# First inverse steps in pairs, wider VectorE steps, one tile for x's two parts and a reload by halves, in a newly planned order

## The chip, the cores and the metric

The kernel runs on one core of a Trainium2 chip. The time is device time in microseconds for one execution; the profile of one execution, taken by the hardware profiler, gives its span and the start and duration of its instructions. In the profile PE is TensorE, DVE is VectorE, ACT is ScalarE, POOL is GpSimd and SP is SyncE.

## The reference

Two heads are computed from inputs of 2048 positions and 512 channels and put side by side.

```python
def _A_ref(x, dft_seq_re, dft_seq_im, dft_hid_re, dft_hid_im):
    a = einsum("bsd,ed->bse", x, dft_hid_re)
    b = einsum("bsd,ed->bse", x, dft_hid_im)
    return einsum("ts,bse->bte", dft_seq_re, a) - einsum("ts,bse->bte", dft_seq_im, b)

def _B_ref(u, log_A_real, A_imag, C_real, C_imag, log_dt, D_skip):
    dt = exp(log_dt); A = -exp(log_A_real) + 1j * A_imag
    C = (C_real + 1j * C_imag) * dt[:, None]
    P = exp((A * dt[:, None])[:, :, None] * arange(L)[None, None, :])
    K = 2.0 * einsum("dn,dnl->dl", C, P).real
    y = irfft(rfft(u_t, 2 * L) * rfft(K, 2 * L), 2 * L)[:, :, :L]
    return transpose(y) + u * D_skip
```

The first head is a Fourier mixing of x by four given matrices. The second convolves each channel of u with a kernel K that is a sum of 128 complex exponentials.

## The kernel before, in words

**Fnet** (the first head) works in 12 groups. Eight groups ("s") multiply x, transposed, with a block of the sequence matrices (the input `in_sT`), 16 items of 128 rows each, into four PSUM tiles `acc` of 128x512; the results `p` go to memory and come back. Four groups ("p") multiply the hidden matrices `w` with `p`, 8 items each. Every operand is fp32 and is split into a high part `hi` (a copy rounded to fp32r, on ScalarE, L233) and a low part `lo` (the difference, on VectorE, L238), and every product is made of three matmuls, high by high, low by high and high by low: 1920 matmuls at L405. x and w stay in SBUF, both parts; a block arrives as `raw` (L346 on ScalarE's queue for the very first, L350 on SyncE's for the others) and is split when it is due. At the end of a group, ScalarE copies `acc` into `y` (L419; L414 for the last), and a DMA stores it.

**Ssm** (the second head) uses two more PSUM tiles, `f0` and `f1`, for everything it does:

- Tables of exponentials, `t` (t1 and t2), in 16 chunks of 32 channels. Each is doubled step by step: VectorE multiplies the part there is by a factor (`mul`, L641, real and imaginary products into `prod`), and adds the two (`add`, L650).
- Taps (L838, 16 steps) multiply t1 by t2 into K. Stage 1 of the transform of K (L893, 8 steps) and of u (L956, 8 steps) go to memory.
- Quarters: four parts of 128 channels (h = 0 to 3), each with four quarters of the frequencies (q). One quarter is a stage-1 step (L1085, into both `f` tiles), ScalarE's copy of them into the tile `uk` (L1064), VectorE's products of the two spectra (L1069 and L1071, then the difference L1102 and the sum L1105), and the first inverse (L1112) into both `f` tiles, from which ScalarE copies into `z` (L1139, L1158). Two DMAs store each z to `zs`.
- When all quarters of a part h are stored, `zs` comes back as `zl`, and the second inverse follows: `inverse` (L1255) for h = 0 and 1, `inverse2` (L1216) for 2 and 3, with a sum and a difference on VectorE ahead of it (L1207, L1209). Its result goes out as `out_yb` (L1241).

For h < 3 the first inverse was made for one quarter at a time (32 matmuls), for h = 3 for two at a time (64 matmuls, `first_inverses`).

**The order.** Nothing is scheduled by the compiler: a planner written in Python (`Plan`) runs when the kernel is built. Each part of the work is a generator that asks for an engine with a cost in us and an urgency, or waits for an event or a semaphore. The planner gives the engine to the request that can start first, and instructions are emitted in that order on every engine. Its costs are the constants `HOP` (from one engine to another), `RESULT` and `LATENCY` (of a DMA), and the functions `act`, `dve` and `load`. Engines execute in order, so an instruction that waits holds those behind it on its engine. Of a DMA, it is the issue that stands in an engine's order: SyncE issues most of them, and ScalarE a few. DMAs of these two take turns on eight completion semaphores, so an issue also waits until the one eight issues earlier has landed.

Of the kernel before, what the change touches and what calls it, by code (L numbers as in the profile page):

```python
# [54 lines left out]
HOP, RESULT, LATENCY = 0.3, 0.15, 3.3  # L55
# [34 lines left out]
class Plan:  # L90
# [3 lines left out]
    def __init__(self):  # L94
        self.free, self.ready, self.now = {}, [], 0.0
        self.count, self.streaming = 0, True
        self.done, self.blocks, self.asked = 0, [], -9.0

        self.later, self.ticks = [], []

    def spawn(self, gen, urgency=0, at=None):
        self.step([self.now if at is None else at, urgency, self.count, gen, None, None], None)
        self.count += 1

    def step(self, p, value):
        self.now = p[0]
        while True:
# [15 lines left out]
            else:  # L123
                if r[0] != p[5]:
                    p[0] += HOP
                elif r[0] == "dve" and len(r) < 4:
                    p[0] += RESULT
                p[4], p[5] = r, r[0]
                self.ready.append(p)
# [3 lines left out]
    def set(self, ev):  # L133
        ev.time = self.now
        self.wake(ev.waiting)
# [8 lines left out]
    def wake(self, procs):  # L144
        now = self.now
        for p in procs:
            p[0] = max(p[0], now)
# [3 lines left out]
    def key(self, p):  # L151
# [4 lines left out]
        return int(start / GRAIN), urgency[0]() if urgency and urgency[0] else p[1], start, p[2]  # L156
# [16 lines left out]
    def run(self):  # L173

        while self.ready:
# [12 lines left out]
            p[0] = start + dur + (LATENCY if engine.startswith("dma") else 0.0)  # L188
# [15 lines left out]
class Fnet:  # L204
# [51 lines left out]
    def still(self, k):  # L256
        return [self.pool.tile([128, DM], F32R, name=f"x_{m}{k}") for m in ("hi", "lo")]

    def spare(self, k, shape):
        return [self.pool.tile(shape, F32, name=f"x_{m}{k}") for m in ("hi", "lo")]  # L260
# [8 lines left out]
    def load_x0(self, raw):  # L269
# [9 lines left out]
        self.plan.set(self.x0_ev)  # L279

    def load_x1(self, b, raw, n):
# [11 lines left out]
        self.plan.set(self.x_ev[n])  # L293
# [33 lines left out]
    def load_soft(self, src, i):  # L327
# [12 lines left out]
        self.plan.set(self.m_ev[i])  # L340

    def load(self, src, to, where, key, ev):
# [5 lines left out]
        else:  # L348
            yield "dma", load(256)
# [9 lines left out]
        self.plan.set(ev)  # L359

    def matmuls(self):
        for g in self.groups:
            still_ev = self.x_ev if g[0] == "s" else self.w_ev
            items, acc = self.items[g], []
            for batch in [[i] for i in items[:-BATCH]] + [items[-BATCH:]]:
                steps = self.steps(g, batch)
                for d in range(4):
# [3 lines left out]
                    for i in batch:  # L371
# [8 lines left out]
                        for t in self.plan.ticks[:]:  # L380
                            t[0] -= 1
                            if not t[0]:
                                self.plan.ticks.remove(t)
                                self.plan.set(t[1])
# [55 lines left out]
class Joined(Event):  # L440


    def __init__(self, ssm, run):
        super().__init__()
        self.ssm, self.fn, self.got = ssm, run, None

    def run(self, got, shared=True):
        self.got, self.users = got, {k: 1 for k, _ in got}
        if shared:
            self.users[got[0][0]] = 2  # L450
        self.fn(got)

    def leave(self, k):
        self.users[k] -= 1
        if not self.users[k]:
# [816 lines left out]
ZS = 1, 4  # L1272
# [78 lines left out]
```

## Time and profile before

| | before |
|---|---|
| time, median of 3 runs | 573.72 us (573.46 to 574.24) |
| the profiled execution: time | 574.7 us |
| the profiled execution: span | 572.9 us, 15632 instructions |
| granted TensorE clock | 0.999 |
| DMA | 133.70 MB, mean 233 GB/s |
| ACT | 371.1 us busy, 65% of the span |

The span runs from the first to the last instruction that the profile shows; the time of the same execution is 1.8 us longer, for what lies around it. A row of the timeline is: start in us, duration in us, engine, line, operation, output tile <- inputs, shapes, how many; in brackets the idle time in front of it and what ended it. "ACTq" and "SPq" are DMA issues on those engines' queues. A row of groups is: line, engine, operation, tiles, shapes, count, then busy us in all and mean ns of one, then idle time in front. A row of the chain is: start, duration, engine, tile, line, number of matmuls. A row of the DMA issues ends with the KB of one and the median us from issue to landing. In the slices of the page one digit is the busy share of a fortieth of the span, in tenths. A row of windows gives the stretch and its length, then the busy us of PE, PEld, DVE, ACT and POOL with their instructions, then the granted clock, the DMA share and GB/s.

### The profile page before, as it was taken

The numbers are of one execution on the slowest core, as the hardware profiler recorded it, in microseconds if no ns is written. First come the engines' busy times: TensorE is split into PE (matmuls) and PEld (weight loads), VectorE is DVE, ScalarE is ACT, GpSimd is POOL, SyncE is SP. The second block draws the span as 40 slices with busy tenths as digits, with TensorE's granted clock in tenths as the row PEclk, the third lists the DMA queues.
The fourth block names the chain that finished last, engine by engine and source line by source line (L and its number), as shares of the span: only waits on it lengthen the run. The fifth ranks groups of instructions, "written<-read, shape, count | busy, mean of one in ns | idle before, by whom it ended". The sixth has DMA issues, their size and how long they took to land. (4 is left out here: it accounts for less than half of the span.)

```text
span 572.9 us, 15632 instructions
## 1 busy us (share of the span) xinstructions
PE 563.6 (98%) x6278; PEld 432.5 (75%) x6278; DVE 517.7 (90%) x909; ACT 371.1 (65%) x734; POOL 40.3 (7%) x60
## 2 busy tenths in 40 slices
PE   8999999999999999999999999999999999999996
PEld 6777766888877777778787777777787778776784
DVE  7999999999999999999999999999999999464731
ACT  5889765663777595858669486845588844354433
POOL 0000000110110000100101001001100000000000
PEclk9999999999999999999999999999999999999999
DMA  8999999997559768767696788569999997589994
GB/s 259 322 368 269 289 291 262 289 282 188 134 149 233 203 183 234 195 172 229 181 248 200 223 210 246 144 162 273 283 295 256 227 284 224 127 255 266 277 253 148
DMA packets 147976, 133.70 MB, mean 233 GB/s; under 512 B 47296, under 2 KB 107328, under 8 KB 147648
## 3 DMA queue, kind: packets, MB, share of 16 engines
q1 hardware_dynamic: 138976, 115.54, 67.5%
q0 software_dynamic: 8064, 14.68, 12.9%
q10 hardware_dynamic: 864, 2.49, 1.8%
q8 instruction: 49, 0.80, 0.6%
q14 instruction: 23, 0.19, 0.1%
HBM read 89.95 MB, written 42.73 MB: 232 GB/s over the span
## 5 line engine op out<-in xcount | busy, mean ns | idle before, releaser
L405 PE MATMUL acc<-hi,x_lo 128*128 128x512 f32 x640 | 251.6, 393 | 0.0
L405 PE MATMUL acc<-hi,x_hi 128*128 128x512 f32 x640 | 247.6, 396 | 0.0
L405 PE MATMUL acc<-lo,x_hi 128*128 128x512 f32 x640 | 192.5, 393 | 0.1
L641 DVE TENSOR_TENSOR prod<-t,cs 128x1024 f32<-128x1024 f32 (+4 forms) x192 | 163.1, 868 | 1.8 <-ACT t L758 0.6
L405 PEld LDWEIGHTS acc<-hi,x_hi 128*128 128x128 f32 x640 | 120.1, 188 | 36.8 <-issue 11.1
L405 PEld LDWEIGHTS acc<-lo,x_hi 128*128 128x128 f32 x640 | 118.9, 188 | 32.0 <-issue 6.5
L405 PEld LDWEIGHTS acc<-hi,x_lo 128*128 128x128 f32 x640 | 120.2, 188 | 29.0 <-issue 5.0
L238 DVE TENSOR_TENSOR lo<-raw,hi 128x512 fp32r<-128x512 f32 x132 | 90.0, 685 | 27.0 <-ACT hi L233 16.2
L233 ACT ACTIVATE hi<-raw 128x512 fp32r<-128x512 f32 x132 | 82.3, 626 | 45.7 <-PE acc L405 35.5
L650 DVE TENSOR_TENSOR t<-prod 128x512 f32<-128x512 f32 (+4 forms) x192 | 94.1, 511 | 1.0
L657 ACT ACTIVATE square<-t 128x256 f32<-128x256 f32 (+1 forms) x64 | 36.8, 575 | 38.2 <-DVE t L650 34.8
L336 POOL DMA_DIRECT2D lo<-in_sT x28 | 24.3, 869 | 227.0 <-ACT lo L334 58.1
L419 ACT ACTIVATE y<-acc 128x512 f32<-128x512 f32 x47 | 28.0, 595 | 16.5 <-PE acc L405 16.4
L1064 ACT ACTIVATE uk<-f 128x1024 f32<-128x1024 f32 x32 | 31.1, 1017 | 11.4 <-PE f L1085 9.4
L838 PEld LDWEIGHTS f<-t,t 128*32 128x32 f32 x2048 | 29.4, 110 | 6.6 <-issue 4.2
L838 PE MATMUL f<-t,t 128*32 128x64 f32 x2048 | 32.0, 220 | 0.8 <-DVE zl L974 0.8
L331 POOL DMA_DIRECT2D hi<-in_sT x28 | 16.3, 582 | 171.9 <-PE acc L405 58.5
L670 DVE TENSOR_TENSOR t<-square 128x128 f32<-128x128 f32 (+1 forms) x64 | 24.6, 385 | 0.0
L1085 PE MATMUL f<-xt,w 64*32 64x256 f32 x768 | 23.5, 379 | 0.5 <-DMA xt<-xk 0.5
L852 ACT ACTIVATE ks<-f 128x512 f32<-128x512 f32 x16 | 9.6, 597 | 21.5 <-PE f L838 21.5
L1071 DVE TENSOR_TENSOR uk<-uk 128x512 f32<-128x512 f32 x32 | 22.1, 691 | 0.9
L1069 DVE TENSOR_TENSOR z<-uk 128x512 f32<-128x512 f32 x32 | 21.9, 684 | 1.0 <-ACT uk L1064 0.6
(105 smaller groups left out, 503.1 us busy)
## 6 DMA issues: line engine op xcount, KB each, us to landing
raw<-in_sT SPq DMA_DIRECT2D x99, 256.0 KB, 5.4
p<-y SPq DMA_DIRECT2D x32, 256.0 KB, 3.4
xk<-xk_sb SPq DMA_DIRECT2D x32, 256.0 KB, 5.2
zs<-z SPq DMA_DIRECT2D x32, 256.0 KB, 4.1
raw<-p SPq DMA_DIRECT2D x32, 256.0 KB, 5.2
hi<-in_sT POOLq DMA_DIRECT2D x28, 256.0 KB, 5.1
lo<-in_sT POOLq DMA_DIRECT2D x28, 256.0 KB, 5.0
xt<-xu SPq DMA_DIRECT2D x24, 256.0 KB, 5.0
```

The lines of the kernel that those rows point to most:

```text
L233: self.nc.scalar.activation(hi, src, AF.Copy)
L238: self.nc.vector.tensor_tensor(lo, src, hi.bitcast(F32), op=OP.subtract)
L336: self.nc.gpsimd.dma_start(lo, src, accum_op=OP.add)
L405: self.nc.tensor.matmul(acc[d], still["hl".index(p[0])][:, 128 * d:128 * d + 128], m["hl".index(p[1])], start=i is items[0] and p == "hh", ...
L419: self.nc.scalar.activation(y, ps, AF.Copy, scale=-1.0 if g[2] == 1 else 1.0)
L641: self.nc.vector.tensor_tensor(p.rearrange("p k d c m -> p k (d c) m"), src.rearrange("p d c l -> p (d c) l")[:, None, :, rows].to_broadca ...
L650: self.nc.vector.tensor_tensor(dst[:, :, :, rows], p[:, 0], p[:, 1, :, ::-1], op=OP.add)
L657: self.nc.scalar.activation(sq, t[:, :, :, m // 2:m], AF.Square)
L670: self.nc.vector.tensor_tensor(t[:, :, 0, m:2 * m:2], box[0][:, :, 0], box[0][:, :, 1], op=OP.subtract)
L838: nc.tensor.matmul(ps[32 * j:32 * j + 32, i], t1[:, d, c], t2[:, d, c], start=c == 0, stop=c == 1, tile_position=(0, 32 * j))
L1064: a.activation(uk[:, r].rearrange("p g c n d -> p g (c n d)"), p, AF.Copy)
L1085: nc.tensor.matmul(got[r][1][32 * xx:32 * xx + 32, g, 256 * c:256 * c + 256], self.w2[rows, 2 * q + r, xx, 32 * c:32 * c + 32], xt[rows].r ...
```

## The change

1. **Pairs.** `first_inverses` now serves all parts: two quarters of a part wait for each other, and their first inverses are one step of 64 matmuls (L1132 now). For h < 3, the difference and the sum that feed it are written into the tile that held the products (`z`, two of them instead of one), so `uk` is free earlier. The class that joined single inverses to other steps, and the list of steps set behind the products in progress, are gone.
2. **Wider VectorE steps.** The last doubling of each table chunk was made in two halves (a product of 1024 columns and a sum of 512, twice); now there are two products of 1024 and one sum of 1024 (`whole`, `join`). In the quarters h < 3, four products of 512 become two of 1024, which need both copies of `uk`.
3. **x in one tile.** The high and low parts of x share a tile, and when it is reused for spectra of h = 3, each reload is one DMA of 256 KB instead of two of 128.
4. **Reload by halves.** In `inverse2`, `zl` is fetched by two DMAs of 256 KB per half of the partitions instead of one of 512, and each half waits only for its two quarters. ScalarE's queue now issues eight such DMAs, SyncE's eight.
5. **Tiles shared.** `f1u` uses a corner of `ia`'s tile (`ia` is then loaded later, `const3_ev`), and `ib2` takes over `ib`'s.
6. **The planner.** `HOP_PE` (0.5) for steps that go to PE, `LATENCY_0` (2.3) for the first 8 us, other rates for some loads, and two tables, `SHIFT` and `HOLD`, that move the urgency or the earliest start of single requests. The order is new on all engines.

Three places of the order. In these rows, `raw` is a block as it arrives, `uk` at the start holds a block of x as it arrives, and the number behind a tile's name tells tiles apart.

At the start, SyncE's order before was x's first 128 columns, the rest of them, and so on; `raw_131` on ScalarE's queue is item 0, `raw_132` item 1:

```order
L272 DMA uk_130<-in_x 128x128
L284 DMA uk_130<-in_x 128x384
L284 DMA uk_130<-in_x 128x512
L350 DMA raw_132<-in_sT 128x512
L284 DMA uk_130<-in_x 128x512
L350 DMA raw_133<-in_sT 128x512
```

SyncE's order now, where `raw_132` is item 2 and `raw_131` item 1:

```order
L377 DMA raw_132<-in_sT 128x512
L299 DMA uk_129<-in_x 128x128
L311 DMA uk_129<-in_x 128x384
L311 DMA uk_129<-in_x 128x512
L377 DMA raw_131<-in_sT 128x512
L311 DMA uk_129<-in_x 128x512
```

ScalarE's order there, before:

```order
L346 DMA raw_131<-in_sT 128x512
L233 ACT_TABLE_LOAD
L233 ACTIVATE hi_147<-raw_131 128x512
L233 ACTIVATE x_hi0_140<-uk_130 128x384
L233 ACTIVATE x_hi1_150<-uk_130 128x512
```

And now, with `raw_130` as item 0:

```order
L373 DMA raw_130<-in_sT 128x512
L259 ACT_TABLE_LOAD
L259 ACTIVATE hi_138<-raw_132 128x512
L259 ACTIVATE hi_142<-raw_130 128x512
L259 ACTIVATE x0_145<-uk_129 128x384
L259 ACTIVATE x1_151<-uk_129 128x512
```

Item 2 has moved ahead of x on SyncE and ahead of item 0 on ScalarE.

ScalarE among the quarters of h = 3, where h = 2 comes back as `zl`. Before:

```order
L1064 ACTIVATE uk_6805<-f0_6804 128x1024
L233 ACTIVATE hi_6860<-raw_6581 128x512
L1200 DMA zl_6683<-zs_107 64x2x1024
L1200 DMA zl_6684<-zs_107 64x2x1024
L233 ACTIVATE hi_6886<-raw_6627 128x512
L1158 ACTIVATE z_6939<-f1_6897 128x2x2x128
L1158 ACTIVATE z_6939<-f0_6898 128x2x2x128
```

Now (two more of these issues stand a little ahead):

```order
L1163 ACTIVATE z_6795<-f0_6755 128x2x2x128
L1163 ACTIVATE z_6795<-f1_6756 128x2x2x128
L1208 DMA zl_6670<-zs_107 64x1024
L259 ACTIVATE hi_6825<-raw_6511 128x512
L1069 ACTIVATE uk_6821<-f0_6813 128x1024
L1069 ACTIVATE uk_6821<-f1_6820 128x1024
L1208 DMA zl_6671<-zs_107 64x1024
L1069 ACTIVATE uk_6877<-f0_6867 128x1024
L1069 ACTIVATE uk_6877<-f1_6876 128x1024
L259 ACTIVATE hi_6931<-raw_6531 128x512
L1208 DMA zl_6874<-zs_107 64x1024
```

The issues are twice as many, and single ones stand between the copies of `uk` (L1069 now) and `z` (L1163 now).

The end of PE's order before, where the second inverse of h = 3 reads `zsum` and `zl`:

```order
L1216 MATMUL f0_7438<-zsum_7351,ib2_6665 32x128 x2
L1216 MATMUL f0_7438<-zl_7298,ib2_6665 32x128 x2
L405 MATMUL acc_7214<-hi_7327,x_hi6_5722 128x512
L405 MATMUL acc_7214<-hi_7327,x_lo6_5723 128x512
L405 MATMUL acc_7214<-hi_7345,x_hi7_5759 128x512
L405 MATMUL acc_7214<-hi_7345,x_lo7_5760 128x512
L405 MATMUL acc_7214<-lo_7328,x_hi6_5722 128x512
L405 MATMUL acc_7214<-lo_7346,x_hi7_5759 128x512
```

And now, where the rows of the inverse (L1224 now) go on to the end of the program:

```order
L427 MATMUL acc_7140<-hi_7184,x6_5441 128x512 x2
L427 MATMUL acc_7140<-hi_7202,x7_5481 128x512 x2
L427 MATMUL acc_7140<-lo_7185,x6_5441 128x512
L427 MATMUL acc_7140<-lo_7203,x7_5481 128x512
L1224 MATMUL f1_7307<-zsum_7231,ib_113 32x128 x2
L1224 MATMUL f1_7307<-zl_7148,ib_113 32x128 x2
```

The last second inverse has moved from six products ahead of the end to behind the last product. On ScalarE the last `acc` is now copied ahead of this inverse's result.

The core of the diff:

```diff
-HOP, RESULT, LATENCY = 0.3, 0.15, 3.3
+HOP, HOP_PE, RESULT, LATENCY, LATENCY_0 = 0.3, 0.5, 0.15, 3.3, 2.3
+SHIFT = {
...
+    ('load', ('p', 3, None, 7), 0): 4, ('load', ('s', 0, 0, 2), 0): -0.6, ('load', ('s', 1, 0, 10), 1): 1,
...
+        shift = SHIFT.get(p[6], 0.0) + SHIFT.get((*p[6], p[7] - 1), 0.0)
...
-    def halves(self, name, t, rows, seed, to):
-        for d in (slice(0, CHUNK // 2), slice(CHUNK // 2, CHUNK)):
-            p = yield from self.mul(name, t[:, d], rows, seed[:, :, d])
-            yield from self.add(p, t[:, d], to)
+    def whole(self, name, t, rows, seed, to):
+        n = 2 * CHUNK * len(range(64)[rows])
+        p = self.tab.tile([128, 1024], F32, name=name)[:, :n].rearrange("p (d c m) -> p d c m", d=CHUNK, c=2)
+        for k, dst in enumerate((t[:, :, :, to], p)):
+            yield "dve", dve(n), *APART
+            self.nc.vector.tensor_tensor(dst, t[:, :, :, rows],
+                                         seed[:, k, :, :, None].to_broadcast([128, CHUNK, 2, n // 2 // CHUNK]), op=OP.mult)
+        return p
+    def join(self, p, dst, *apart):
+        yield "dve", dve(2 * p.shape[1] * p.shape[3]), *apart
+        self.nc.vector.tensor_tensor(dst, dst, p[:, :, ::-1], op=OP.add)
...
-            yield "dve", dve(512)
+            if h == 3:
+                yield from both(slice(r, r + 1))
+            left[0] -= 1
+            if left[0]:
+                return
+            if h < 3:
+                yield from both(slice(0, 2))
+            self.plan.set(ready)
...
+        pair = self.pair[h]
+        pair.append((q, run))
+        if len(pair) == 2:
+            yield from self.first_inverses(b, h, pair.pop(0), pair.pop(0))
...
-        nc.scalar.dma_start(z[64:], view[:, :, n * i + c:n * i + n])
-        yield "dma", load(64 * n, 270), FAST if h == 3 else None
-        nc.sync.dma_start(z[:64], view[:, :, n * i:n * i + c])
+        for a in range(2):
+            yield self.zs_ev[h][a]
+            yield "act", 0.5
+            nc.scalar.dma_start(z[64:, a], view[:, a, n * i + c:n * i + n])
+            yield "dma", load(32 * n, 270 if h == 3 else 170), FAST if h == 3 else None
+            nc.sync.dma_start(z[:64, a], view[:, a, n * i:n * i + c])
...
-BEHIND = {("k", 0), ("k", 1), ("u", 2), ("u", 3), ("u", 4), ("u", 5), ("t", 12), (0, 0), (0, 2), (1, 2)}
-BEHIND_L = 3
-ZS = 1, 4
+BEHIND = set()
+ZS = 2, 4
```

More of the change, by code (lines that the diff above doesn't have):

```diff
@@ L131, in step, with set @@
             self.now = p[0]
-    def set(self, ev):
-        ev.time = self.now
-        self.wake(ev.waiting)
+    def set(self, ev, after=0.0):
+        ev.time = self.now + after
+        self.wake(ev.waiting, ev.time)
         ev.waiting = []
@@ L437, in __init__ @@
         self.xts, self.uks, self.zbs, self.zls = Sem(1), Sem(n), Sem(self.zn), Sem(2 * n - 1)
[L440 to L455, printed above, removed]
-            self.ssm.give(k)
 class Ssm:
@@ L472, in __init__ @@
         first = ("f1u", f1u), ("f1k", f1k), ("dskip", dsk)
[L473 to L474 removed]
+        second, third = (("w2", w2), ("ib", ib)), (("ia", ia),)
+        tiles = {n: self.const.tile([128, *a.shape[1:]], F32, name=n) for n, a in (*first[1:], *second, *third)}
+        tiles["f1u"] = tiles["ia"][:, 0, 0]
+        self.cst = [[(n, tiles[n], a) for n, a in s] for s in (first, second, third)]
         self.halfpi = self.const.tile([128, 1], F32, name="halfpi")
@@ L845, in taps @@
         self.plan.put(self.t2s)
-        self.taps_left -= 1
-        if other:
-            self.plan.set(other)
-        while self.waiting and not self.taps_left:
-            self.plan.set(self.waiting.pop(0))
         yield "act", act(512)
@@ L1002, in quarters @@
         self.ib2_ev, self.loaded_ev = Event(), Event()
-        self.pair, self.last, self.k_ev = [], [], Event()
+        self.pair, self.last, self.k_ev = [[] for _ in range(4)], [], Event()
         self.plan.spawn(self.load_ib2(), 1)
@@ L1093, in product @@
         self.plan.set(done)
+        for r in range(h == 3, 2):
+            self.plan.spawn(half(r, *got[r]), urgency)
         yield b.zbs
@@ L1146, in first_inverses, with products @@
+        pair = self.pair[h]
+        pair.append((q, run))
+        if len(pair) == 2:
+            yield from self.first_inverses(b, h, pair.pop(0), pair.pop(0))
+    def first_inverses(self, b, h, *two):
+        yield self.const3_ev
+        if (h, two[1][0]) == (2, 3):
+            yield self.k_ev
         got = yield from self.banks(2)
         yield "pe", 1.05 + 0.87, None, 128
-        for n, (q, run) in enumerate(two):
-            run(got, 2 * PART * n)
-            self.plan.put(b.uks)
+        def products():
+            for n, (q, run) in enumerate(two):
+                run(got, 2 * PART * n)
+        if (h, two[0][0]) in BEHIND:
+            self.plan.later.append(products)
+        else:
+            products()
```

183 lines of the change are left out of this document (85 added, 98 removed), and 3 rows, old and new, of the table SHIFT.

## The prediction

> **What bounds the kernel now.** I read the page first, then PE's timeline, the chain and PE's waits. On the page, the busy times and DVE's slices:
>
> ```profile
> PE 563.6 (98%) x6278; PEld 432.5 (75%) x6278; DVE 517.7 (90%) x909; ACT 371.1 (65%) x734; POOL 40.3 (7%) x60
> DVE  7999999999999999999999999999999999464731
> ```
>
> TensorE works 563.6 of 572.9 us. VectorE is as full as it for most of the run, but its last seven slices are half empty, while PE has no empty stretch. So PE sets the time, and the others count only where PE waits for them. What PE does is a stream of Fnet's products into `acc`, interrupted by steps into `f0`/`f1` for the convolution. Its timeline shows what one interruption costs:
>
> ```profile
> 487.84 0.39 PE L405 MATMUL acc<-hi,x_lo 128*128 128x512 f32 x1
> 488.16 1.12 PE L893 MATMUL f<-ks,f1k 32*64 32x256 f32 x32
> 489.21 0.50 PE L405 MATMUL acc<-hi,x_hi 128*128 128x512 f32 x1
> 489.55 0.39 PE L405 MATMUL acc<-hi,x_lo 128*128 128x512 f32 x1
> ...
> 493.52 1.12 PE L1112 MATMUL f<-uk,ia 32*64 32x256 f32 x32
> 494.57 0.50 PE L405 MATMUL acc<-hi,x_hi 128*128 128x512 f32 x1
> ```
>
> The chain of waits, in order of time, gives the lengths of the other steps that the change touches and the pitch of the stream:
>
> ```profile
> 535.61 1.91 PE f L1112 x64
> ...
> 545.22 13.82 PE acc L405 x60
> 559.04 1.09 PE f L1216 x64
> ```
>
> Sixty products take 13.82 us with one return in front, (13.82 - 0.1)/60 = 0.228 each. The last product before the step at 488.16 takes 0.32 to the next start and the first one after it 0.34 (489.21 to 489.55), where 0.228 is normal: **an interruption costs 0.09 + 0.11 = 0.2 us on top of its own work.** A single first inverse is 1.05 (493.52 to 494.57), a pair 1.91.
>
> The stream runs from 4.55 to 567.41 (both quoted below), 562.86 us. Its 1920 products at 0.228 are 437.8, the 68 interruptions 13.6, and the own work of the 71 steps in them about 105 (from 1.05 to 2.0 each, as in the rows above, added up over the timeline; this can be off by 1). About 6 to 7 us are left, in which PE waits. The waits view names less than half of it, the rest lies in starts that slip by 0.2 to 0.5:
>
> ```profile
> PE f L838 <- DVE zl L974: 0.8, 1, 0.8
> PE f L1085 <- ACT z L1158: 0.8, 1, 0.8
> PE f L1112 <- DVE uk L1102: 0.5, 2, 0.3
> PE f L1085 <- DMA xt<-xk: 0.5, 1, 0.5
> ```
>
> (total, times, longest.) So there are three ways to a shorter time: less work in the stream, fewer interruptions, and the 6 to 7 us of waits. Before the stream lie 4.55 us and behind its last start 5.5.
>
> **The change, part by part.**
>
> *Pairs.* Twelve single first inverses become six pairs: 6 x 1.91 - 12 x 1.05 = -1.1. Six interruptions fewer: 6 x 0.2 = -1.2. The work hidden beside them does not change: ScalarE copies the same columns, and the stores are as many.
>
> *The last second inverse* leaves the stream: it stands behind the last product in the new order. That takes 1.09 out of the stream, **-1.1**. The stream is 3.4 shorter in all. What follows the stream gets longer. The tail of before, then the landing times from the list of DMA issues:
>
> ```profile
> 565.06 0.30 PE L1216 MATMUL f<-zsum,ib 64*32 64x128 f32 x2
> ...
> 567.18 0.62 PE L405 MATMUL acc<-lo,x_hi 128*128 128x512 f32 x2
> 567.39 0.38 SPq L1241 DMA_DIRECT2D out_yb<-zl  x1
> ...
> 568.47 0.37 ACTq L416 DMA_DIRECT2D out_ya<-y  x1
> ```
>
> ```profile
> out_yb<-zl SPq DMA_DIRECT2D x8, 512.0 KB, 4.3
> out_ya<-y ACTq DMA_DIRECT2D x1, 128.0 KB, 3.2
> ```
>
> Before, the last product starts at 567.18 + 0.23 = 567.41, `out_ya` is issued 1.06 later, lands 3.2 after that, and 1.2 more pass to the end of the span: 5.5. From the start of the last second inverse (565.06) to the issue of its `out_yb` (567.39) are 2.33. If it starts 0.3 behind the last product, the end is 0.3 + 2.33 + 4.3 + 1.2 = 8.1 behind it; with the last of the eight landings alone, 3.3 by the trace, 7.1. So +1.6 to +2.6; I take **+2.0**, nearer the middle because the queue is empty then. Nothing is left to hide it: behind the last product PE has no other work.
>
> *The start.* SyncE's first transfer is now item 2's 256 KB of `sT`, ahead of the 64 KB of x (ScalarE still fetches item 0's 256 KB), and ScalarE splits item 2 before item 0, which the first product needs. Before:
>
> ```profile
> 3.87 0.63 ACT L233 ACTIVATE hi<-raw 128x512 fp32r<-128x512 f32 x1 [1.41 <-DMA raw<-in_sT]
> ...
> 4.41 1.27 ACT L233 ACTIVATE x_hi<-uk 128x384 fp32r<-128x384 f32 x2
> ...
> 4.55 0.55 PE L405 MATMUL acc<-hi,x_hi 128*128 128x512 f32 x1
> ```
>
> ```profile
> 3.00:4.00 1.00, 1.00 (x4) 0.67 (x2) 0.33 (x2) 0.13 (x1) 0.00 (x0) 1.00 1.01 380
> ```
>
> ScalarE's next split starts 0.54 behind the first (3.87 to 4.41). One split more ahead of item 0 is therefore +0.54 at least. In the window from 3 to 4 us (last two columns: DMA share 1.01, 380 GB/s) the transfers already fill all engines. If they share that rate, 512 KB instead of 320 KB must land first: 192 KB / 380 = 0.5 later. Both together are +1.04, and VectorE's low part of item 2, also put first, holds the third product a little longer. Bounds +0.5 and +1.3; I take **+1.2**.
>
> The Trainium skill speaks to this in "DMA: Bandwidth & Descriptors", section "Issuing engines are not separate DMA queues": transfers started by different engines run on the same 16 DMA engines and interleave. The planner in the code lets ScalarE's transfer run on a lane of its own. By the page the start is +1.2, by the planner's assumption +0.54; the window above, with all engines full at 380 GB/s, agrees with the page.
>
> *Wider VectorE steps.* The groups:
>
> ```profile
> L641 DVE TENSOR_TENSOR prod<-t,cs 128x1024 f32<-128x1024 f32 x96 | 116.6, 1219 | 0.7
> L650 DVE TENSOR_TENSOR t<-prod 128x512 f32<-128x512 f32 x96 | 65.2, 685 | 0.5
> L1069 DVE TENSOR_TENSOR z<-uk 128x512 f32<-128x512 f32 x32 | 21.9, 684 | 1.0 <-ACT uk L1064 0.6 <-DMA x_hi<-xk 0.3
> ```
>
> A doubled step takes 1.22 where two take 1.37. In the tables, 32 sums are joined: 32 x 0.15 = 4.8 us. In the quarters h < 3, 24 pairs of products: 24 x 0.15 = 3.6. So VectorE does 8.4 us less. PE hides it, and by itself it is worth nothing. It costs something too: the wide product waits for both ScalarE copies, so 2 x 1.22 = 2.44 stand behind the second copy instead of 1.37, 1.1 us later to the inverse. A pair waits for its second quarter anyway, and in the new order stands 24 to 36 products (5.5 to 8.2 us) behind the stage-1 step of it. If that cover were too short, each of the eight pairs would wait up to 1.1.
>
> *One tile for x's two parts, z's reload by halves, shared constant tiles.* The bytes are the same. SyncE and ScalarE issue at 0.4 us each, beside the stream, so I cost them at 0 where they stand; where ScalarE is held by its own issue is the second rival.
>
> *The waits.* The order is new everywhere, so old waits go and new ones come. The one at 522 us shows what a wait is made of:
>
> ```profile
> 520.26 0.58 ACTq L1200 DMA_DIRECT2D zl<-zs  x1
> 520.97 0.63 ACT L233 ACTIVATE hi<-raw 128x512 fp32r<-128x512 f32 x1 [7.44 <-PE acc L405]
> 521.50 2.04 ACT L1158 ACTIVATE z<-f 128x512 f32<-128x512 f32 x4
> ```
>
> ScalarE did nothing for 7.44 us; its next instruction in order was the reload at 520.26, and the copies of z that free PSUM stood behind it. PE's next stage-1 step came 0.8 late (the second row of the waits). Bounds: 0 if new waits make up for all, -6 if all go. I take the sum of the four named rows, **-2.6** (0.8 + 0.8 + 0.5 + 0.5), nearer to nothing than to all: 8.4 us less on VectorE and fewer PSUM hand-overs help, but the slips that no row names have no reason to go.
>
> *Sum:* -3.4 + 2.0 + 1.2 - 2.6 = **-2.8**. Against the profiled run that is a span of 570.1 and a time of 571.9 instead of 574.7; that run was 1.0 above the median. From the median of 573.72 it gives **570.9 us**.
>
> **Rivals.**
>
> *The waits stay* (each old one has a new one in its place). For it: PE waits about 1% of the time in an order that was also planned, by costs that know no slipping starts. Against it: less VectorE work, fewer stops. -3.4 + 3.2 = -0.2: 573.5 us, no difference.
>
> *The reload holds ScalarE*: slower. Reloads of h = 2 and 3 on ScalarE's queue are now eight instead of four, issued between the copies that free PSUM. It decides when the transfer that an issue waits for is under way longer than about 6 us, which is what passes in the new order between a quarter's store and the first reload of it:
>
> ```profile
> zl<-zs ACTq DMA_DIRECT2D x4, 512.0 KB, 8.0
> zs<-z SPq DMA_DIRECT2D x32, 256.0 KB, 4.1
> ```
>
> The store's median of 4.1 speaks against it, the reload's 8.0 us for it: the queues are full there. Four of the eight late by 0.9, the price seen at 522: +3.6 - 0.2 = +3.4, 577 us.
>
> *Nearly all waits go*: -0.2 - 6 = 567.5. VectorE's emptier slices would speak for it, but the first and third rows of the waits, those on VectorE, lie where it is at 9 tenths, and 8.4 us of 517.7 do not empty it there.
>
> *The change does not do what it says*: the order rules that out for pairs and tail; both stand where the sum has them.
>
> **How the numbers follow.** A measurement of this kernel can tell about 0.2%, 1.15 us, from no change. Forecast (-1.15 to -5.5, so 568.2 to 572.6): 0.58. Waits stay: 0.18. ScalarE held: 0.14. Nearly all waits go: 0.10. Faster 0.68, same 0.18, slower 0.14. The range goes from 567.2, in the middle of the fourth case, to 575.0, which takes in the third case's mild end with one or two held reloads (573.5 + 2 x 0.9); out of it is less than 0.2.
>
> **What would show it.** Start: the first product at 5.0 to 5.9. Pairs: eight rows of the first inverse with 64 matmuls at about 1.91, and 62 interruptions ahead of the last product. Tail: the last second inverse behind the last product, and 7.1 to 8.1 from that product's start to the end. Waits: the remainder of the stream at 3 to 5 us instead of 6 to 7. Wrong would be a remainder above 7, a ScalarE row with several us of idle time before a copy into `uk` or `z`, or pairs that wait for `uk`.

## The result and the profile after

| | before | after |
|---|---|---|
| time, median of 9 runs each, same chip | 574.21 us (573.46 to 576.16) | 577.96 us (576.94 to 580.75) |
| ratio | 1 | 1.0068, 95% interval 1.0050 to 1.0086 |
| the profiled execution: time | 574.7 us | 577.05 us |
| the profiled execution: span | 572.9 us | 575.3 us, 15562 instructions |

The change makes the kernel slower by 0.68%, about 3.8 us. A gain was forecast, to 570.9, with a range from 567.2 to 575.0.

The page of after, busy times and VectorE's slices, and then from the groups PE's first inverses that now come in pairs (h < 3):

```profile
PE 562.2 (98%) x6278; PEld 434.6 (76%) x6278; DVE 514.8 (89%) x853; ACT 372.2 (65%) x734; POOL 40.3 (7%) x60
DVE  5989999999999999999999999999999999555841
```

```profile
L1132 PE MATMUL f<-z,ia 32*64 32x256 f32 x384 | 12.4, 381 | 0.0
```

VectorE has 56 instructions fewer, as it should (909 to 853), and 2.9 us less busy time where 8.4 were worked out. It is as full as before. No pair is late to start (last column 0.0). One of the eight is slower inside: from its start to the next product are 2.47 us, where the other seven take 1.91. By the profile, most of its weight loads waited for ScalarE's copies into `uk`, which ended at 214.93:

```profile
214.42 2.54 PE L1132 MATMUL f<-z,ia 32*64 32x256 f32 x64
```

PE's waits in after (total, times, longest), to be read beside the four rows shown of before; a row for the warm-up, the same in both, and two of 0.2 are left out:

```profile
PE acc L427 <- issue: 1.6, 1, 1.6
PE acc L427 <- ACT hi L259: 1.3, 1, 1.3
PE f L1098 <- DMA xt<-xk: 1.3, 1, 1.3
PE f L897 <- DVE ks L869: 0.5, 2, 0.3
PE f L850 <- issue: 0.5, 1, 0.5
PE f L960 <- DVE zl L978: 0.5, 1, 0.5
```

Before, the longest was 0.8. Now there are three of 1.3 or more, and "issue", in which PE waited for nothing that the profile shows, is the first of them. The three places in the timeline of after, at the start, at 408 and at 430 us:

```profile
4.62 1.15 ACT L259 ACTIVATE hi<-raw 128x512 fp32r<-128x512 f32 x2 [2.17 <-DMA raw<-in_sT]
5.82 1.22 PE L427 MATMUL acc<-hi,x 128*128 128x512 f32 x2 [1.32 <-ACT hi L259]
6.84 0.78 PE L427 MATMUL acc<-lo,x 128*128 128x512 f32 x1
...
408.00 2.02 PE L1098 MATMUL f<-xt,w 64*32 64x256 f32 x64 [1.28 <-DMA xt<-xk]
...
429.30 1.52 PE L427 MATMUL acc<-hi,x 128*128 128x512 f32 x6
432.41 0.62 PE L427 MATMUL acc<-hi,x 128*128 128x512 f32 x2 [1.59 <-issue]
```

And the end of after:

```profile
568.02 0.61 PE L427 MATMUL acc<-lo,x 128*128 128x512 f32 x2
568.56 0.30 PE L1224 MATMUL f<-zsum,ib 64*32 64x128 f32 x2
...
570.90 0.38 SPq L1245 DMA_DIRECT2D out_yb<-zl  x1
```

A ledger of the two profiled executions, worked out as in the prediction (products at 0.2275, 0.2 for an interruption, each step by its usual length; what is left of the stretch is PE's waiting, and what it loses while its clock is low counts in it):

| us | before | after | difference |
|---|---|---|---|
| up to the first product | 4.55 | 5.82 | +1.27 |
| the stream's own work | | | -3.4 |
| waits in the stream | 6.8 | 9.8 | +3.0 |
| last product's start to the end of the span | 5.50 | 7.03 | +1.5 |
| span | 572.9 | 575.3 | +2.4 |

So three of the four terms are near where the prediction had them. The waits rose by 3.0 where they were to fall by 2.6. The medians differ by 1.4 more than the profiled executions do; a second profile of the changed kernel, the first one below, is longer by 1.7.

### The profile page after: what moved, and what is told of

Same layout as the page of the kernel before. It is cut to its first block, busy times and chain, and to the rows that moved or that the text cites. A ratio compares the mean times of both kernels' runs of the same rounds, so it can differ in the third digit from the quotient of the medians.

```text
span 575.3 us, 15562 instructions
## 1 busy us (share of the span) xinstructions
PE 562.2 (98%) x6278; PEld 434.6 (76%) x6278; DVE 514.8 (89%) x853; ACT 372.2 (65%) x734; POOL 40.3 (7%) x60
## 4 chain that ended last, share of the span: by engine, by line
PE 67%; DVE 17%; DMA 8%; issue 5%; ACT 2%; SPq 0%; ACTq 0%; DVEq 0%
PE acc L427 52%; PE f L1098 5%; PE f L850 4%; DMA raw<-in_sT 4%; DVE lo L264 3%; DVE prod L646 3%; PE f L1132 3%; DVE t L655 2%; DVE t L757 2%; DVE prod L757 2%; PE f L897 2%; PE f L1259 1%; DMA xu<-z 1%; DMA cs<-in_ldt 1%; DMA uk<-in_x 1%
## 5 line engine op out<-in xcount | busy, mean ns | idle before, releaser
L427 PE MATMUL acc<-hi,x 128*128 128x512 f32 x1280 | 344.4, 396 | 2.9 <-issue 1.6
L427 PEld LDWEIGHTS acc<-hi,x 128*128 128x128 f32 x1280 | 237.1, 188 | 69.9 <-issue 17.3
L427 PE MATMUL acc<-lo,x 128*128 128x512 f32 x640 | 191.0, 392 | 0.0
L427 PEld LDWEIGHTS acc<-lo,x 128*128 128x128 f32 x640 | 119.7, 188 | 29.3 <-issue 4.0
L646 DVE TENSOR_TENSOR prod<-t,cs 128x128 f32<-128x128 f32 (+4 forms) x128 | 87.2, 694 | 2.2 <-ACT t L793 1.2
L655 DVE TENSOR_TENSOR t<-prod 128x64 f32<-128x64 f32 (+4 forms) x128 | 52.7, 425 | 0.9
L757 DVE TENSOR_TENSOR t<-t,cs 128x1024 f32<-128x1024 f32 x32 | 39.1, 1221 | 0.3
L763 DVE TENSOR_TENSOR t<-t,prod 128x1024 f32<-128x1024 f32 x32 | 39.0, 1219 | 0.1
L757 DVE TENSOR_TENSOR prod<-t,cs 128x1024 f32<-128x1024 f32 x32 | 38.9, 1217 | 0.0
L1069 ACT ACTIVATE uk<-f 128x1024 f32<-128x1024 f32 x32 | 31.4, 1018 | 10.2 <-PE f L1098 9.7
L1163 ACT ACTIVATE z<-f 128x512 f32<-128x512 f32 x32 | 17.2, 605 | 12.4 <-PE f L1132 12.4
L1085 DVE TENSOR_TENSOR z<-uk 128x1024 f32<-128x1024 f32 (+1 forms) x20 | 20.1, 1005 | 5.4 <-ACT uk L1069 5.3
L1098 PE MATMUL f<-xt,w 64*32 64x256 f32 x768 | 23.5, 379 | 1.3 <-DMA xt<-xk 1.3
```

Of the source, the lines that this page charges most:

```text
L427: self.nc.tensor.matmul(acc[d], still["hl".index(p[0])][:, 128 * d:128 * d + 128], m["hl".index(p[1])], start=i is items[0] and p == "hh", ...
L646: self.nc.vector.tensor_tensor(p.rearrange("p k d c m -> p k (d c) m"), src.rearrange("p d c l -> p (d c) l")[:, None, :, rows].to_broadca ...
L655: self.nc.vector.tensor_tensor(dst[:, :, :, rows], p[:, 0], p[:, 1, :, ::-1], op=OP.add)
L757: self.nc.vector.tensor_tensor(dst, t[:, :, :, rows], seed[:, k, :, :, None].to_broadcast([128, CHUNK, 2, n // 2 // CHUNK]), op=OP.mult)
L763: self.nc.vector.tensor_tensor(dst, dst, p[:, :, ::-1], op=OP.add)
L1069: a.activation(uk[:, r].rearrange("p g c n d -> p g (c n d)"), p, AF.Copy)
```

## The experiments

Most kernels here are the changed kernel with its planned order written out as a list, in which single entries are moved; everything that isn't moved keeps its place on every engine. "Waits" is the ledger's third row in that kernel's profile. The kernel before was timed beside each experiment: 573.8 to 574.7 us. Where two kernels were not timed together, their ratios to it are the fair comparison.

**The changed kernel once more**, planned as it is.

> The changed kernel itself, as the measure for the runs beside it. 577 to 579 us. If the waits of its first profile come from its order, PE shows them again at the same places: the first product at 5.8, the stage-1 step L1098 late by about 1.4 us at product 1398, a stop of about 1.8 us near product 1470 that the profile calls issue. If they are accidents of one execution, they stand elsewhere or are gone.

577.99 us, 1.0064 (1.0052 to 1.0077), the same as in the result. This second profile of it has waits of 11.8. The three long waits are there again, at the first product (1.0 instead of 1.3), at 410 us (0.7 instead of 1.3) and at 434 us:

```profile
PE acc L427 <- issue: 1.5, 1, 1.5
```

So they belong to this order. A fourth came: PE stopped at 44 us as well, and then ran slowly. The timeline, and windows of 6 us (third column from the end: the granted clock):

```profile
42.85 1.09 PE L960 MATMUL f<-xt,ia 32*64 32x512 f32 x8
45.25 1.76 PE L960 MATMUL f<-xt,ia 32*64 32x512 f32 x8 [1.31 <-DVE zl L978]
46.94 1.65 PE L427 MATMUL acc<-hi,x 128*128 128x512 f32 x3
```

```profile
42.00:48.00 6.00, 4.69 (x24) 1.73 (x23) 5.93 (x14) 4.51 (x11) 0.00 (x0) 0.79 1.02 370
48.00:54.00 6.00, 6.00 (x19) 4.73 (x18) 4.14 (x11) 3.54 (x10) 0.00 (x0) 0.64 0.33 124
```

A step of 1.09 takes 1.76 behind the stop, and the clock is at half for 6.8 us in all, so up to 3.4 of the 11.8 are slow running.

**Each visible wait taken away alone.** First the start: item 2's fetch and both its splits go behind x's third block, as they stood in the kernel before.

```diff
 SyncE:
-L377 DMA raw<-in_sT 128x512        (item 2)
 L299 DMA uk<-in_x 128x128
 L311 DMA uk<-in_x 128x384
 L311 DMA uk<-in_x 128x512
+L377 DMA raw<-in_sT 128x512        (item 2)
```

> The changed kernel with its order kept row by row, but item 2 of sT is fetched, split and subtracted behind x2's block, as in the kernel before, on SyncE, ScalarE and VectorE. Theory A (the waits are the order's own): the first product goes from 5.8 back to 4.6 us and the slow first products (1.1 us) go too, so -2.0 to -2.5 us against the changed kernel. Theory B (VectorE sets the pace of the first 90 us): PE is earlier, but waits longer at L960 and L850 before 90 us, so -0.5 to +0.5 us in the end.

The first product came at 4.58, as before, and the time didn't move: 578.15, 1.0066 (1.0048 to 1.0083). In the profile the gain was lost again at 43 us, where a wait of 1.9 stood instead of 0.5 and 1.3 in the two profiles above:

```profile
PE f L960 <- DVE zl L978: 1.9, 1, 1.9
```

PE arrived earlier at a step whose input VectorE still had to make. In that execution the clock went down there too, for 3.4 us.

**The stop at 430 us.** PE's instructions come in blocks of 16 KB (256 of them) over a queue of their own. In the window from 424 to 432 us the transfers filled all engines (DMA share 1.00, the last column but one), and one block was in it (the view of the DMA queues: packets, MB, share of the engines):

```profile
424.00:432.00 8.00, 6.82 (x149) 5.49 (x148) 8.00 (x16) 6.23 (x16) 1.43 (x2) 1.00 1.00 265
```

```profile
q8 instruction: 1, 0.02, 0.7%
```

SyncE had issued a large load just ahead of it:

```profile
423.49 0.61 SPq L1195 DMA_DIRECT2D ib<-in_ib  x1
```

That block landed at 431.11, and PE went on 1.3 us later. The 512 KB of `ib2` issued at 423.49 are needed near 520, so this load goes eleven SyncE rows later:

```diff
 SyncE:
-L1195 DMA ib<-in_ib 128x1024
 L377 DMA raw<-p 128x512
...
 L377 DMA raw<-p 128x512
+L1195 DMA ib<-in_ib 128x1024
 L377 DMA raw<-p 128x512
```

> The changed kernel with its order kept, but the 512 KB load of ib2, which it issues at 423.5 us and needs at about 520, is issued some ten SyncE rows later. Theory A with PE's instruction fetch as the cause of the stop at 430 us (the 16 KB packets of the instruction queue come 6.4 us after PE has used 150 instructions of the block before, where 0.6 to 4 us are usual): the lag falls to 5 us or less, the stop shrinks from 1.8 to under 0.7 us, and the time by 1 to 1.8 us. Rival: the stop has another cause (a semaphore, a split that the profile does not name): it stays, and so does the time within 0.5 us.

576.36, 1.0034 (1.0022 to 1.0046): 1.6 less than the changed kernel's 577.99. In the same window the DMA share is 0.80 and PE works 7.59 us instead of 6.82; of the stop 0.3 is left:

```profile
424.00:432.00 8.00, 7.59 (x152) 6.09 (x151) 8.00 (x15) 6.71 (x18) 1.42 (x2) 1.00 0.80 189
```

```profile
PE acc L427 <- issue: 0.3, 1, 0.3
```

The lag of 6.4 us that the expectation goes by is no mark by itself: by the same count the next block of that profile has 6.3, and PE did not stop for it. And in the profile of e_fetch PE also came to the place 1.0 us later, which shortens the stop by itself; the block landed at 430.50, 0.6 earlier. All the profiles together are clearer: in the six that issue the load at the old place (after, its second profile, e_start, e_warm, e_u, e_su) PE stops here for 1.2 to 1.6 us, in the seven that issue it later (e_fetch, c0, c1, c2, c_tail, c_split, c_light) for 0 to 0.3. And in the 18 profiles that can be read PE has 25 stops called "issue", each of which ends 1.2 to 1.6 us after a block of instructions landed. So a late block is what "issue" means here. This is the one wait whose removal alone paid.

**The wait at 408 us**: the stage-1 step (L1098) of h = 2 goes six products later.

> The changed kernel with its order kept, but the first stage-1 step of h = 2 (L1098) stands six products later, behind the landing of its spectrum. Theory A: the wait of 1.3 us for xt is filled with products, -1.0 to -1.4 us. Rival: what follows from that step is itself the next bound (its copies, the inverse): the wait comes back behind it, within 0.4 us of the changed kernel.

578.17, 1.0066 (1.0053 to 1.0079): nothing. Its profiled execution has a span of 3157.8 us and says nothing here. But c1 and c2 below make the same move. There the wait at 408 us is gone, and one for a sum of VectorE's stands at 426 us, of 0.9 in c1 and 0.6 in c2, where c0 has none (c_tail, without the move, has 0.7 and 0.5 at the two places). The row of c1:

```profile
426.08 1.11 PE L850 MATMUL f<-t,t 128*32 128x64 f32 x65 [0.91 <-DVE t L763]
```

**A longer warm-up**: one matmul more ahead of the first product (`range(3)` to `range(4)` in `warm`, L279).

> The changed kernel with its order kept and one more fp32 matmul of zeros (two passes) ahead of the first product, so that TensorE is idle for some 0.3 to 0.8 us before it instead of 1.3. The clock records of the runs so far show half the clock from 7.8 to 11.2 us in one run and up to 8.9 in another, and none after 4.6 in a third. Theory C (an idle stretch of more than about a microsecond lets the granted clock fall to half for 3.4 us, at random from run to run): the first products follow at 0.23 from at most the fifth on, no record of half clock between 5 and 12 us, -0.5 to -1.5 us in the median. Rival (the start is set by the split alone): no change, within 0.4 us.

577.47, 1.0052 (1.0033 to 1.0072): -0.5, within the noise of the two.

**The wait at 45 us**: VectorE's two sums for u (L976, L978) go four rows earlier.

> The changed kernel with its order kept, but VectorE's two steps (L976, L978) that free the second f tile for the second stage-1 step of u stand four rows earlier, ahead of table work. Theory C: the wait of 1.0 to 1.3 us inside that step at 43 us goes, and with it the half clock for 3.4 to 6.8 us that two of four runs show right behind it: -1.0 to -3.0 us in the median, no half clock between 40 and 60 us. Theory B (VectorE is the bound there): the wait moves to the next step, 0 to -0.5 us.

577.98, 1.0065 (1.0045 to 1.0084): nothing. The wait at 45 us was gone, and two waits, 0.6 at 55.75 us and 0.4 at 57.76, stood behind it, for an `acc` that ScalarE copies behind the load of a table.

**Start and u together, and with the load of `ib2`** (kernel c0).

> Both: the start in the order of before, and VectorE's two steps of u earlier. The start alone gave nothing (578.15 against 577.99), and its trace shows a longer wait at 43 us (1.9 instead of 1.3) and half clock for 3.4 us behind it. Theory C: with that wait gone the start's 1.2 us come through, -3.0 to -4.5 us against the changed kernel, 573.5 to 575.0. Theory B: no more than e_u alone.

> The three moves together: start, VectorE's two steps, and ib2 loaded later (which alone gave -1.6). If they are independent, -4.6 to -6.0 us against the changed kernel: 572.0 to 573.4, below the kernel before by 0.2 to 0.4%. If they share a bound, no better than the best of them.

The two together: 576.87, 1.0040 (1.0025 to 1.0054), -1.1 where 3.0 to 4.5 were expected. All three: 576.06, 1.0031 (1.0022 to 1.0041), -1.9 where 4.6 to 6 were expected. The waits that were aimed at went, others came: 10.0 in the ledger. So a wait's length is not what its removal is worth here; something else holds PE nearly as late. The candidate is VectorE. Windows of before, then of c0, 90 to 240 and 240 to 400 us (the third number behind the length is VectorE's busy time):

```profile
90.00:240.00 150.00, 149.29 (x1591) 116.65 (x1597) 148.66 (x266) 99.86 (x203) 15.71 (x22) 1.00 0.78 208
240.00:400.00 160.00, 159.75 (x2015) 123.59 (x2007) 158.45 (x278) 107.85 (x219) 16.23 (x23) 1.00 0.77 210
```

```profile
90.00:240.00 150.00, 148.75 (x1735) 114.90 (x1724) 145.82 (x246) 98.99 (x204) 14.87 (x21) 1.00 0.78 210
240.00:400.00 160.00, 160.00 (x1946) 125.97 (x1946) 158.31 (x257) 112.65 (x230) 15.75 (x22) 1.00 0.77 207
```

It is idle for 1 to 3 us in each 100, before and after. Five experiments ask what that means.

**VectorE's wide steps undone in c0's order**: both halves in place of each wide step, 56 instructions more.

```diff
-            p = yield from self.whole("prod", t, slice(0, 16), cs[:, :, 10], slice(16, 32))
-            yield from self.join(p, t[:, :, :, 16:32])
+            for d in (slice(0, CHUNK // 2), slice(CHUNK // 2, CHUNK)):
+                yield from self.add((yield from self.mul("prod", t[:, d], ..., cs[:, :, 10, d])), t[:, d], ...)
...
-                yield from both(slice(0, 2))
+                for s in range(2): yield from both(slice(s, s + 1))
```

> The kernel c0 (576.06) with its order, but VectorE's wide steps undone: the last doubling of each table in two halves (a product of 1024 and a sum of 512, twice) and the products of the quarters h < 3 in four steps of 512, 56 more steps and 8.4 us more of VectorE's time. Theory as in the prediction (PE hides it): within 0.8 us of c0. Theory B (VectorE sets the pace until 480 us): +3 to +8 us.

587.30, 1.0222 (1.0207 to 1.0237): +11.2. Its profile has 22.4 us of waits, and the view of waits begins with VectorE; the page's busy times ahead of it:

```profile
PE 566.8 (97%) x6278; PEld 436.0 (74%) x6278; DVE 524.4 (89%) x909; ACT 371.8 (63%) x734; POOL 40.3 (7%) x60
```

```profile
PE f L897 <- DVE ks L869: 4.8, 5, 1.7
PE f L1098 <- DMA xt<-xk: 2.4, 1, 2.4
```

PE does not hide VectorE's work in this order. The order had been planned for the wide form, so the 11.2 is not what wide steps are worth.

**Work taken from VectorE in c0**: in 8 of 16 chunks the last sum of t1 is left out, 8 steps of 1.14 us, so the output lacks these sums.

```diff
-            yield from self.join(p, t[:, :, :, 16:32])
+            if n % 2 == 0: yield from self.join(p, t[:, :, :, 16:32])
```

> c0 (576.06) with its order, but the last sum of t1 (L763, 1024 columns, 1.14 us from start to start) is left out in eight of the sixteen chunks, so these tables hold half of the sum in their upper half: 9.1 us less for VectorE, the same for all others. Theory B (VectorE sets the pace while it is full, until 480 us; doing more, in c_narrow, cost 11): -3 to -8 us. Theory A (PE's own waits set it, VectorE has slack): -1 to 0 us.

573.69, 0.9983 (0.9973 to 0.9994): 2.4 less than c0 by the medians, 2.8 by the ratios, for 9.1 us less work on VectorE. The waits fell from 10.0 to 6.5, and the one at 408 us, which the profile puts down to a DMA, is gone.

**The same in the kernel before**, in its own order: in 4 of 16 chunks both products of t1's last doubling are left out.

```diff
     def halves(self, name, t, rows, seed, to, full):
         for d in (slice(0, CHUNK // 2), slice(CHUNK // 2, CHUNK)):
+            if not full:
+                yield "dve", dve(1024); yield "dve", dve(512)
+                self.nc.vector.tensor_tensor(t[:, d, :, to], t[:, d, :, rows], t[:, d, ::-1, rows], op=OP.add)
+                continue
```

> The kernel before in its own order, but in 4 of 16 chunks both products of t1's last doubling are left out (8 VectorE steps of 1024 columns; the sum is made of t1 itself, so the output is not the reference's): 8 x 1.14 = 9.1 us less VectorE, as much as the kernel c_light left out of the changed kernel for 2.4 us. Theory B1 (VectorE bounds the kernel before just as it bounds the changed one): -1.5 to -4 us against the kernel before. Theory B2 (VectorE was covered before, and the changed order lost that cover): -0.7 to +0.5 us.

571.41 against 573.81, 0.9955 (0.9940 to 0.9971): 2.4 less again, 2.6 by the ratio. PE's waits fell from 6.8 to 2.7. This is all that its view of waits still names besides the warm-up:

```profile
PE f L1112 <- DVE uk L1102: 0.3, 1, 0.3
```

So VectorE held PE in the kernel before as well, by about the same 0.26 us per us of its work (0.2 to 0.4 by the intervals), although only two short rows of its waits, 0.8 and 0.5, name it. Whether it held PE by its load or by tables that were ready too late, the two experiments don't tell apart: leaving steps out changes both.

**The tables' wide steps alone, in the order of the kernel before**: the two products and the sum stand where the first product, the second product and the last sum stood; 32 instructions fewer.

> The kernel before in its own order, with the change's wide VectorE steps in the tables alone (the last doublings of t1 and t2: two products of 1024 and one sum of 1024 at the places of the first product, the second product and the last sum; 32 steps fewer, 32 x 0.07 = 2.2 us less VectorE). Theory B1 (VectorE binds in part, and b_light gained 0.26 us per us taken out): -0.4 to -1.1 us against the kernel before. Prediction's theory (VectorE is covered): -0.2 to +0.2. Theory W (the wide form delays the tables, since the first half is no longer ready early, and this costs PE more than the saving): +0.5 us or more.

574.64 against 574.22, 1.0010 (0.9998 to 1.0023): no gain, where B1 had 0.4 to 1.1. The view of waits has two new rows, one for the sum (L799) that is now made only once, at the end, and one called "issue", at 486 us:

```profile
PE f L838 <- issue: 1.0, 1, 1.0
PE f L838 <- DVE t L799: 0.8, 2, 0.6
PE f L838 <- DVE zl L974: 0.8, 1, 0.8
```

The row for L799 is what Theory W expects: a wide step's first half is no longer ready early. But the profile doesn't settle that this gave the saving back. The 1.0 at 486 us is a late block of instructions, the first 12 products lost 1.0 more than in the profile of before, and between products 216 and 1300 the waits are smaller, 3.0 instead of 4.2. One execution can't say how much of this is chance, so why there was no gain stays open.

**Order alone**: the changed kernel planned without the two tables of shifts (`SHIFT, HOLD = {}, {}`).

> The changed kernel without its two tables of shifts: the same steps and planner costs in another order. If the order alone decides several us, it differs from the changed kernel (577.99) by more than 1.5 us, more likely slower, 580 to 586. If the steps set the time, it is within 1 us.

590.22, 1.0280 (1.0263 to 1.0296): +12.2 with the same work. The products ended 4 us earlier than in the kernel before, and PE then waited at the end:

```profile
PE f L1224 <- DVE zsum L1215: 10.5, 1, 10.5
```

**The pairs, taken apart in c0**: the six new pairs become singles again with three products between.

```diff
-        yield "pe", 1.05 + 0.87, None, 128
+        for n, (q, run) in enumerate(two):
+            if h < 3 or not n:
+                yield "pe", 1.05, None, 64
+            run(got, 2 * PART * n)
```

> c0 with its order, but each of the six new pairs is taken apart again: 32 matmuls for the first quarter, three products, 32 for the second (the same f tiles, the same copies behind them). Theory as in the prediction (a pair saves 2 x 1.05 - 1.91 = 0.19 and an interruption of 0.2): 6 x 0.39 = +2.3 us. Rival (PE waits anyway, the saving is lost in waits): +0 to +0.8.

577.91, 1.0061 (1.0046 to 1.0076): +1.85 against c0, by the intervals some 0.7 to 2.7. That agrees with the 2.3 that the rows say. In the timeline, one pair taken apart; it is the one with the slow place inside, and its first half takes 1.65 to the next row instead of 1.05:

```profile
215.23 1.72 PE L1132 MATMUL f<-z,ia 32*64 32x256 f32 x32
216.88 0.73 PE L427 MATMUL acc<-hi,x 128*128 128x512 f32 x2
217.46 0.39 PE L427 MATMUL acc<-lo,x 128*128 128x512 f32 x1
217.77 1.12 PE L1132 MATMUL f<-z,ia 32*64 32x256 f32 x32
```

**The last second inverse** back ahead of the last six products, in c0.

> Kernel c0 with the last second inverse back ahead of the last six products, where the kernel before had it; nothing else moved. By the prediction (-1.3 in the stream, tail +1.5 as measured in the profile): the tail is 5.5 again and the stream 1.3 longer, so -0.2 us against c0 (574.5 to 577.5 against 576.1). If the two do not offset each other (the stored result lands later than the profile's 4.3 us): -1 us or more.

576.49 against 573.81, 1.0043 (1.0029 to 1.0057), where c0 has 1.0031 (1.0022 to 1.0041): the intervals overlap, and the move pays little or nothing. The tail in its profile is 6.1, not 5.5.

**More moves on c0** (c1): the last second inverse ahead of the last six products as in c_tail, VectorE's and ScalarE's rows for u between 43 and 56 us earlier, a table load of ScalarE's at 53 us later, and the stage-1 step at 408 later.

> c0 with four more rows moved: the copy and the two VectorE steps that free f for the second step of u directly behind the first ones (c0 waits 1.0 us there); the copies of the first acc tiles at 53 us ahead of a table load of ScalarE (c0 waits 1.0); the first stage-1 step of h = 2 six products later (1.3); the last second inverse six products ahead of the end, as before (the tail 1.5 shorter, the stream 1.3 longer). Theory A (the waits are the order's own): -2.5 to -3.7 us against c0, 572.4 to 573.6, below the kernel before (574.5). Theory B (behind each of these waits the next bound stands): -0.5 us or less.

576.14, 1.0035 (1.0022 to 1.0049): nothing, where 2.5 to 3.7 were expected. One copy of `acc` still stood behind the table load, and PE waited for it:

```profile
56.29 0.73 PE L427 MATMUL acc<-hi,x 128*128 128x512 f32 x2 [1.56 <-ACT y L441]
```

**That mended**, the last inverse behind the products again, and its store cut in two (c2).

> c1 without its own fault and with a shorter end: the table load of ScalarE at 53 us stands behind all four copies of acc (in c1 the fourth copy stood behind it and PE waited 1.6 us), the last second inverse stays behind the last product, and its result is stored in two halves, each behind its copy. Theory A: against c0 -1.9 (the waits from product 132 to 216, 3.1 in c0, fall to 1.2), -0.5 (xt), -0.8 (the end, 7.0 in c0): 572.5 to 574.0. Theory B: the end alone comes through, -0.5 to -1.0, 575.1 to 575.6.

575.29, 1.0009 (0.9995 to 1.0023): of the 0.68% that the change had cost, 0.09% is left, not told apart from none. What brought the last 0.2% against c0 was not taken apart. No version that does the whole work beat the kernel before.

## Why the prediction was wrong

- **Start, +1.2: right.** The first product came at 5.82 instead of 4.55, +1.27 (5.47 in the second profile, +0.92). That the products behind it would run slowly at first (1.02 for two, from 5.82 to 6.84) was not foreseen; the waits of the first 12 products are 1.6 instead of 0.4. And by itself the term was worth nothing: with the old start back, the time stayed (e_start).
- **Pairs, -2.3: right.** Eight steps with 64 matmuls and no wait in front, and 1.85 when six of them were taken apart. One pair lost 0.6 to ScalarE's copies into `uk`, which the prediction had named as a sign of being wrong.
- **Tail, +2.0: mis-sized, +1.5.** From the last product's start, 568.25, to the issue of `out_yb` are 2.65 and from there to the end 4.37, 7.03 in all; the result landed in 3.2, not 4.3, so the trace's mild end (7.1) was the right one. With the 1.1 out of the stream the move is worth about nothing, which c_tail agrees with.
- **Wider VectorE steps, 8.4 us less: mis-sized, 4.0.** The sum took the rows' durations, 2 x 0.685 - 1.22 = 0.15. But consecutive steps overlap:

```profile
403.47 0.68 DVE L264 TENSOR_TENSOR lo<-raw,hi 128x512 fp32r<-128x512 f32 x1
404.07 0.68 DVE L655 TENSOR_TENSOR t<-prod 128x512 f32<-128x512 f32 x1
404.79 1.23 DVE L757 TENSOR_TENSOR t<-t,cs 128x1024 f32<-128x1024 f32 x1
405.93 1.22 DVE L757 TENSOR_TENSOR prod<-t,cs 128x1024 f32<-128x1024 f32 x1
```

  From start to start it is 0.60 for 512 columns (403.47 to 404.07) and 1.14 for 1024 (404.79 to 405.93); over all such neighbours in the trace 0.604 and 1.136. A merged step saves 2 x 0.604 - 1.136 = 0.07, and 56 of them 4.0.
- **"PE hides it, and by itself it is worth nothing": the result held, the reason didn't.** VectorE's work is not hidden, in either kernel: 9.1 us less gave 2.4 in both. By that slope 4.0 us would have been worth 1.1. In the tables alone the wide form brought no gain (b_wide: +0.4, from -0.1 to +1.3). That its first half is ready later may have cost the rest, but that is not shown.
- **Waits, -2.6: this is the step that failed.** The prediction let the four named rows go and set the waits that a new order brings at nothing. The same ledger by stretches of the stream shows both sides (sums differ from the ledger's by up to 0.1):

| waits in us, up to product | 12 (8 to 10 us) | 216 (60 to 64 us) | 1300 (376 to 380 us) | 1500 (441 to 443 us) | 1920 | sum |
|---|---|---|---|---|---|---|
| before | 0.4 | 0.9 | 4.2 | 0.2 | 1.1 | 6.8 |
| after | 1.6 | 1.3 | 3.2 | 3.3 | 0.3 | 9.7 |
| after, second profile | 0.7 | 5.4 | 2.8 | 2.6 | 0.3 | 11.8 |

  In the third and fifth stretch the waits did fall, by 1.8 and 2.2, not far from 2.6. In the other three new ones came, 4.7 and 7.2 in sum: the slow first products, the stop at 44 us with the low clock behind it, the spectrum that landed late at 408 us and the instructions that did at 430. So the waits rose by 3.0 in one profile and 5.0 in the other.

  The old rows were not defects of their own places either. With 9.1 us less work on VectorE all four shrink or go (b_light), also the two that name ScalarE and a DMA: they were where PE met an engine that is full all the time. Of the new ones, the wait at 408 us went in the same way (c_light); the late instructions have nothing to do with VectorE. Moving waits away one at a time gave nothing in three cases of five (start, 408 us, u), -0.5 within the noise in one (the warm-up), and -1.6 in one (the fetch at 430 us). All moves together (c2) brought back 0.59 of the 0.68%, with the same work but for one store cut in two. So it was the new order more than the new steps that made the kernel slower.
- **The rivals.** "The waits stay" was nearest in kind, but waits can also grow, and none of the rivals gave that a price. "The reload holds ScalarE" had 577 us, close to the 577.96 measured, but that is chance: it did not happen. No row of PE's waits names a copy behind a reload, and ScalarE's longest idle time before a copy of `z` or `uk` near the reloads, 4.3 us, is a wait for PE.

**Open:** how much of the 3 us of added waits is this order's own and how much comes from the wide form; and why taking the old start back gave nothing beyond the one profile that shows where it was lost. An order planned anew for the changed kernel without wide steps was not tried, nor the pairs alone in the order of the kernel before. The places at 132 to 216 products (43 to 65 us) kept 2.3 to 3.1 us of waits in c0, c1 and c2, and what holds them there wasn't found.

## What to carry to other kernels

When two engines are both busy above 95% in the same stretch, treat neither as hidden: take a few microseconds of work from the second one, in an order that stays fixed, and measure the slope before pricing its savings. Take the cost of an instruction among its like from start to start, not from its row's duration. And give a new order of the whole program a price for the waits it brings, and a range on both sides: here the order alone, with the same work, was worth 12 us.

## What the runs showed of the hardware

**The clock went down after short stops, in some executions.** The granted clock was halved for 6.8 us from 45.5 us (second profile of the changed kernel), behind an idle PE of 1.3 us; for 3.4 us from 46.9 us with the start moved, behind one of 1.9; twice for 3.4 us in c_narrow, from 45.9 us behind a stop of 0.9 and from 417.9 us within one of 2.4; and not in the profile of after behind its stop of 1.6 at 430 us. In the kernel before it stayed up until 571 us. At the start, the record of the full clock begins at 4.69 us before and at 8.86 in after, but at 4.57 in the second profile of the same kernel, so this part of the slow start differs between executions. In after, most products until then stand 0.43 us apart, and 0.23 behind it. The Trainium skill, "TensorE: Matmul & The Clock Gate", section "Part 1: The HAM clock gate (the "warmup" mystery)", has a free-running window of about 3.4 us and half speed after an idle window. The lengths of 3.4 and 6.8 agree with one and two such windows; that the clock fell with stops of 0.9 to 2.4 us is more than its "≥1 idle window" says. What else decides it is not shown.

**A late block of instructions stopped PE for 1.2 to 1.6 us**, near 430 us in six profiles with a 512 KB load just ahead, and for at most 0.3 in seven without it. The Trainium skill, "Runtime: NRT & Kernel Launch", section "Instruction fetch mechanics", has the fetch in blocks of 16 KB, as seen here, and hidden, which does not hold for this stretch of short matmuls.
